# One fixed order for the whole opening, with half-height matmuls in the short convolution and the turns

## The chip, the cores and the metric

The kernel runs on one core of one Trainium2 chip. The metric is the device time of one execution in microseconds; the time of a kernel is the median over its runs. A profiled execution has its own time and a span, from its first to its last instruction.

## The reference

Two layers are applied twice to x (2048 rows, 448 columns, bf16), and then the gradients of all inputs are formed by the chain rule. Layer A turns k by a causal convolution of four taps, multiplies by v, and convolves the result with a filter as long as the sequence (by a Fourier transform of twice the length). Layer B is a feed-forward net with 1792 hidden columns.

```python
def _A_ref(q, k, v, shift_k, ssm_k, ssm_D):
    for t in range(ks):                      # ks = 4
        k_shift = k_shift + k_pad[:, t:t + S, :] * shift_k[:, ks - 1 - t][None, None, :]
    kv = k_shift * v
    ...                                      # y = irfft(rfft(kv) * rfft(ssm_k)), first S rows
    y = y + kv * ssm_D[None, None, :]
    return q * y
def _B_ref(x, w1, w2):
    return silu(x @ w1) @ w2

x = A_q
x = x + _A_ref(_layernorm(x), A_k, A_v, A_shift_k, A_ssm_k, A_ssm_D)
x = x + _B_ref(_layernorm(x), B_w1, B_w2)
x = x + _A_ref(_layernorm(x), A_k, A_v, A_shift_k, A_ssm_k, A_ssm_D)
x = x + _B_ref(_layernorm(x), B_w1, B_w2)
```

Only the factor q differs between the two uses of layer A: y is the same both times, so the kernel computes it once, ahead of everything else.

## The kernel before

Sequence rows lie as n = 16 p + j, with p the partition. `_ssm_prefix`, the opening, computes y's spectrum and its inverse; `Main` runs the layers forward and backward chunk by chunk (four chunks of 512 rows) and `_ssm_suffix` forms the gradients of k, v and the filter. The opening is the subject here. It has these steps:

- Loads, all issued by SyncE at the start: the filter (ksd, K_sb), the Fourier matrix M1sb, k (k_n), v (v_n), the first rows of x (x0c), small matrices Gsb and Gpre.
- Filter K: `k_turn` turns it with TensorE (ps_kt, copied to KAB); `k_stage1` multiplies by M1sb and copies to A1K (a half of KAB); then seven blocks (each 16 squares of 128 x 128) are turned, five by TensorE in half-height transposes (`turn`) and two by DMA transposes; `spec_k` applies the second stage (ps_s) and copies it back. Each of seven pieces of the spectrum (512 KB) is then stored (spec_K) and copied inside KAB with its halves swapped, by DMAs that GpSimd issues.
- kv: k is turned by 64 full-height transposes (ps_kT, copied to kT); `conv` forms the four-tap convolution as matmuls of kT with 112 x 112 diagonal matrices of the taps (diag, made by 16 VectorE operations from skc); ScalarE copies the result to ks, GpSimd stores it (KS_d), VectorE multiplies by v; `stage1_kv` multiplies by M1sb and copies to A1kv.
- Products: seven blocks of A1kv are turned (Z), the second stage is applied (F), VectorE multiplies with both halves of KAB (M, tile pab), TensorE goes back (V, ps_v), and the result is copied over A1kv. The spectrum of kv is stored (spec_KV), and the weights w1sb and w2sb are loaded behind it by GpSimd's queue.

Tiles of PSUM come from one ring of four (tag "A"). `k.bal` picks ScalarE or VectorE for a copy, by loads it keeps. From second-stage step 9 of K on, the order of TensorE, ScalarE, VectorE and GpSimd is written out in the string PRODUCTS: a capital is the step on TensorE (P, Z, F, V), on VectorE (M) or on GpSimd (Q), a small letter is its copy, with `a` for ScalarE and `d` for VectorE. Ahead of that the scheduler of the framework orders each engine's queue, and instructions of one engine run in that order. The transposes of w2 by DMA (w2T) stand on SyncE's queue behind K's two DMA transposes; the inverse matrix (Minvsb) and the first gradient rows (gb) stand behind them.

Behind the opening, `ys` multiplies A1kv by Minvsb (ps_y, 16 rows in 8 pairs, copied to Ysb), and the forward pass begins. In the suffix ksf reads KS_d back for the product of line 1340.

Of the kernel before, what the change touches and what calls it, by code (L numbers as in the profile page):

```python
# [17 lines left out]
P = 128  # L18
S = 2048
D = 448  # L20
# [101 lines left out]
PRODUCTS = """  # L122
P9 P10 P11 P12 p9a p10d p11a P13 p12d P8 p8a Z0 Q5 p13d Z1 z0d Z2 z1a Q6 F0 z2d F1 f0a F2 f1d F3 f2a F4 Q4 M0 F5 f3a Z4
f4a Z6 z4d f5a z6d F8 f8a F9 M1 F12 F13 f9a Z5 M2 f12a V0 z5d f13a Z3 v0a F11 z3yd z3xd F7 f11a M3 F6 f7a F10 V1 M4 f6a
V2 f10a M6 V3 v1a M5 V4 v2a M11 V5 v3a V6 M10 v4a V11 M12 v5a V10 M13 v6a V12 v11a M7 V13 v10a M8 V7 v12a M9 V8 v13a v8d
V9 v7a v9a
# [16 lines left out]
def kernel(  # L143
# [33 lines left out]
    k.KS_d = dram.tile([2, P, J, D // 2], BF16, name="KS_d")  # L177
# [87 lines left out]
def _fft_inv_stage2_half(k, pa, pb, B1, ci, psum, cnd):  # L265
    nc = k.nc
    pv = psum.tile([P, 2, 8, 64], FP32, name="ps_v", **k.pt["v"])
    for i in range(8):
        for src, g, first in ((pa, G_IAC, True), (pb, G_IBC, False)):
            for r in range(2):  # L270
                ri = slice(64 * r, 64 * r + 64)
                nc.tensor.matmul(pv[:, r ^ (ci & 1), i, :], lhsT=src[ri, i * P:(i + 1) * P], rhs=k.Gsb[ri, g, ri], start=first, stop=not first)  # L272
    out = (B1[:, :, 32 * ci:32 * ci + 32].rearrange("p q (i h s) -> p h i q s", h=2, s=2) if cnd
           else B1[:, 8 * ci:8 * ci + 8, :].rearrange("p i (q h s) -> p h i q s", h=2, s=2))
    _copy(nc, k.bal.pick(1024), out, pv[:].rearrange("p h i (q s) -> p h i q s", s=2))
# [43 lines left out]
def _ln_steps(k, pool, c, src, si, n_g):  # L319
# [4 lines left out]
    for tl in range(4):  # L324
        k.tc.keep_in_program_order(nc.vector.bn_stats(out=st[:, tl, :], in_=src(tl)))
# [5 lines left out]
        yield  # L331
    for tl in range(4):
        k.tc.keep_in_program_order(nc.vector.tensor_scalar(out=n_g[:, tl, :], in0=src(tl), scalar1=mv[:, tl, 0:1], scalar2=r[:, tl:tl + 1], op0=ALU.subtract, op1=ALU.mult))
        yield
# [6 lines left out]
def _ssm_prefix(k):  # L341
# [4 lines left out]
    with ExitStack() as es:  # L346
# [6 lines left out]
        k.M1sb = k.wk.tile([P, 16, 2, P], BF16, name="M1sb", tag="WX")  # L353
# [8 lines left out]
        kT = k.wk.tile([DC, 4, ND, 4, 129], BF16, name="kT", tag="W1")  # L362
        w2o = k.wk.tile([P, 2 * S + ND * 4 * DC], BF16, name="ksd", tag="W2")
        ksb = [w2o[:, i * S:(i + 1) * S] for i in range(2)]
        ksb += [_hd(k, [P, S], "K_sb")[:] for i in range(2)]
        diag = w2o[:DC, 2 * S:].rearrange("p (c j d) -> p c j d", c=ND, j=4)
        kn = k.wk.tile([P, J, D], BF16, name="k_n", tag="WY")
        vn = k.wk.tile([P, J, D], BF16, name="v_n", tag="WB")
        skc = spec.tile([DC, ND, 4], FP32, name="skc")
        skb = spec.tile([DC, ND, 4], BF16, name="skb")  # L370
# [3 lines left out]
        nc.scalar.dma_start(out=skb[:], in_=k.A_shift_k.rearrange("(c p) j -> p c j", p=DC))  # L374
        m1f = k.M1sb[:].rearrange("p a c k -> p (a c k)")
        for h in range(2):
            for lo, hi in KPARTS[2 * h:2 * h + 2]:
                nc.sync.dma_start(out=ksb[lo // P][:hi - lo], in_=k.A_ssm_k[lo:hi, :])
            nc.sync.dma_start(out=m1f[:, 2048 * h:2048 * h + 2048], in_=k.m1_h.ap()[:, 2048 * h:2048 * h + 2048])
# [17 lines left out]
        nc.gpsimd.tensor_copy(skc[:], skb[:])  # L397
        def k_turn(lo, hi):
            n = hi - lo
            kview = ksb[lo // P][:n].rearrange("p (n1 n2) -> p n2 n1", n2=16)  # L400
            pt = psum.tile([P, 2, 1024], BF16, name="ps_kt", **a_)
            pv = pt[:, :, 0:8 * n].rearrange("p g (i d) -> p g i d", d=n)
            for i in range(16):
                nc.tensor.transpose(pv[:, i // 8, i % 8, :], kview[:, i, :], k.ident[:n, :n])
            for g, e in enumerate((nc.vector, nc.scalar)):
                last = _copy(nc, e, Kt[:, 8 * g:8 * g + 8, lo:hi], pv[:, g])
                bal.add("act" if g else "dve", 0.9 if g else 0.69)
                if g == 0:
                    k.kt_copy = last

        def k_stage1(lo, hi, pairs):
            for n2 in pairs:
                ps = psum.tile([P, 2, 2, 256], FP32, name="ps_s1", **k.pt["s1"])
                if n2 == 0:
                    nc.vector.tensor_tensor(out=Kt[0:1, 0, lo:hi], in0=Kt[0:1, 0, lo:hi], in1=Drow[:, lo:hi], op=ALU.add)
                for w in range(2):
                    for c in range(2):
                        nc.tensor.matmul(ps[:, w, c, :hi - lo], lhsT=k.M1sb[:, n2 + w, c, :], rhs=Kt[:, n2 + w, lo:hi], start=True, stop=True)
                _copy(nc, bal.pick(4 * (hi - lo)), A1K[:, lo // 2:hi // 2, :, n2:n2 + 2, :].rearrange("p b c w s -> p w c b s"),
                      ps[:, :, :, :hi - lo].rearrange("p w c (b s) -> p w c b s", s=2))  # L420

        for lo, hi in ((0, 256), (256, D)):
            for plo, phi in KPARTS[lo // P:lo // P + 2]:
                k_turn(plo, phi)
# [1015 lines left out]
```

## Time and profile before

| what | value |
|---|---|
| time, median of 3 runs | 695.63 us (693.44 to 697.43) |
| the profiled execution | 692.97 us, span 690.9 us |
| busy share of the span | PE 97%, PEld 52%, DVE 70%, ACT 62%, POOL 15% |
| granted TensorE clock | 0.999 |
| chain that ended last, by engine | PE 64%, DVE 19%, issue 6%, ACT 5%, DMA 3%, POOL 3% |

PE is TensorE, PEld its loading of weights, DVE is VectorE, ACT is ScalarE, POOL is GpSimd, SP is SyncE (SPq: the queue of DMAs that it issues). A row of the groups gives line, engine, operation, out<-in, shape and count, then the busy time in us and the mean of one in ns, then the idle time ahead of it and what ended it. A row of the windows gives for each engine its busy time in the stretch, then the granted clock, the busy share of the DMA engines and GB/s. A row of the DMA issues gives the count, the KB of each and the median us from issue to landing. Matmuls overlap, so for them the busy time of a group divided by its count is the pace, and the mean is the time from start to end of one.

### The profile page before, as it was taken

The page shows a single profiled execution, that of the slowest core. Times are in us where ns is not written, and L with a number is a line of the kernel's source. Part 1 is how long each engine was busy: PE and PEld are TensorE (multiplying, and loading weights), DVE is VectorE, ACT ScalarE, POOL GpSimd, SP SyncE. Part 2 cuts the span into 40 slices and gives each one's busy share as a digit, 9 for nine tenths or more (in the row PEclk, how much of TensorE's full clock was granted, in tenths as well). Part 3 has the DMA queues.
Part 4 walks back from the last instruction along what each step waited for, and adds up shares of the span by engine and source line. Part 5 has one row for each costly group of instructions (what it writes and reads, how often), then busy time and mean ns, then how long its engine had stood idle before and what let it go on. Part 6 is the DMA issues. An engine that isn't in the chain of part 4 may idle for free.

```text
span 690.9 us, 14461 instructions
## 1 busy us (share of the span) xinstructions
PE 669.0 (97%) x5844; PEld 362.1 (52%) x5879; DVE 481.6 (70%) x1131; ACT 429.9 (62%) x522; POOL 104.8 (15%) x177
## 2 busy tenths in 40 slices
PE   8999999899999999999999999999999999999997
PEld 6876745454434444444444444544555555555666
DVE  5779943667889858899478874843936555538992
ACT  5988976878947868669577585223543543554431
POOL 1057310110011100111001000010111211102311
PEclk9999999999999999999999999999999999999999
DMA  8999978179698777597766789949599988957991
GB/s 320 244 316 321 337 203 220 56 191 259 167 265 233 221 182 176 137 253 219 199 157 183 211 231 354 271 142 210 191 249 342 328 285 315 341 190 223 320 310 42
DMA packets 203956, 162.60 MB, mean 235 GB/s; under 512 B 153505, under 2 KB 184244, under 8 KB 203122
## 3 DMA queue, kind: packets, MB, share of 16 engines
q1 hardware_dynamic: 190806, 113.35, 60.2%
q0 software_dynamic: 11088, 39.84, 16.7%
q10 hardware_dynamic: 1996, 8.49, 3.7%
q8 instruction: 46, 0.75, 0.5%
q14 instruction: 20, 0.16, 0.1%
HBM read 66.05 MB, written 54.60 MB: 175 GB/s over the span
## 4 chain that ended last, share of the span: by engine, by line
PE 64%; DVE 19%; issue 6%; ACT 5%; DMA 3%; POOL 3%; POOLq 0%; ACTq 0%
PE ps_d L1082 25%; PE ps_n L872 8%; PE ps_h L674 6%; PE ps_g L674 6%; PE ps_o L834 5%; DVE ln_st L308 2%; DVE lb_v L1030 2%; PE ps_v L272 2%; POOL rstd L313 2%; DMA spec_K<-KAB 1%; DVE n L316 1%; DVE lb_v L1033 1%; DVE lb_v L1034 1%; DVE X L838 1%; PE ps_h L678 1%
## 5 line engine op out<-in xcount | busy, mean ns | idle before, releaser
L1082 PEld LDWEIGHTS <-dstat 128*128 128x128 bf16 x928 | 87.1, 98 | 75.7 <-issue 4.0
L872 PE MATMUL ps_n<-w1T,ghT 128*128 128x448 bf16 x448 | 96.6, 353 | 2.0 <-DVE ghT L857 1.7
L834 PE MATMUL ps_o<-w2sb,aT 128*128 128x448 bf16 x448 | 89.2, 353 | 0.6 <-DVE X L838 0.6
L674 PE MATMUL ps_h<-nT,w1sb 128*128 128x512 bf16 (+1 forms) x410 | 83.5, 336 | 2.2 <-ACT Dall L116 1.0
L116 ACT CAST ghT<-ps_g 128x1024 bf16<-128x1024 f32 (+1 forms) x54 | 48.4, 900 | 58.3 <-PE ps_g L678 47.7
L674 PE MATMUL ps_g<-nT,w2T 128*128 128x512 bf16 x317 | 77.9, 379 | 2.2 <-DVE Dall L117 0.5
L872 PEld LDWEIGHTS <-ghT 128*128 128x128 bf16 x448 | 41.4, 98 | 50.7 <-DVE ghT L857 6.7
L834 PEld LDWEIGHTS <-aT 128*128 128x128 bf16 x448 | 43.2, 98 | 41.1 <-issue 2.7
L674 PEld LDWEIGHTS <-w1sb 128*128 128x128 bf16 x420 | 39.2, 98 | 36.7 <-issue 7.2
L817 ACT ACTIVATE aT<-ps_h 128x1024 bf16<-128x1024 f32 (+1 forms) x48 | 44.2, 921 | 19.1 <-PE ps_h L674 10.2
L1030 DVE SCALAR_TENSOR_TENSOR lb_v<-lb_u,n 128x448 bf16<-128x448 bf16 x60 | 37.2, 620 | 24.5 <-ACT lb_u L876 24.1
L116 ACT CAST Dall<-ps_h 128x1024 bf16<-128x1024 f32 (+2 forms) x60 | 54.3, 904 | 0.0
L313 POOL TENSOR_TENSOR rstd<-ln_ve,mhalf 128x2 f32<-128x2 f32 (+1 forms) x24 | 19.9, 831 | 225.7 <-DVE ln_ve L312 225.7
L674 PEld LDWEIGHTS <-w2T 128*128 128x128 bf16 x336 | 31.3, 98 | 42.1 <-issue 7.2
L827 ACT ACTIVATE Dall<-Dall 128x1024 bf16<-128x1024 bf16 (+1 forms) x48 | 53.2, 1186 | 0.1
L1082 PE MATMUL ps_d<-X,dstat 128*128 128x448 bf16 x224 | 47.6, 353 | 0.0
L1082 PE MATMUL ps_d<-go,dstat 128*128 128x448 bf16 x224 | 47.2, 353 | 0.0
L1082 PE MATMUL ps_d<-n3m,dstat 128*128 128x448 bf16 (+1 forms) x240 | 47.0, 340 | 0.0
L1082 PE MATMUL ps_d<-n1m,dstat 128*128 128x448 bf16 (+1 forms) x240 | 46.5, 340 | 0.0
L876 ACT ACTIVATE lb_u<-ps_n,rstd 128x448 bf16<-128x448 f32 x32 | 20.5, 640 | 28.9 <-PE ps_n L872 24.3
L116 ACT CAST A1g<-ps_v 128x1024 bf16<-128x1024 f32 x14 | 15.0, 1069 | 36.5 <-PE ps_v L272 36.5
L838 DVE TENSOR_TENSOR X<-X,ps_o 128x448 bf16<-128x448 bf16 x32 | 19.5, 611 | 21.3 <-PE ps_o L834 21.1
(210 smaller groups left out, 1112.4 us busy)
## 6 DMA issues: line engine op xcount, KB each, us to landing
dstat<-a_d SPq DMA_DIRECT2D x28, 512.0 KB, 5.2
dstat<-g_d SPq DMA_DIRECT2D x28, 512.0 KB, 5.8
a_d<-turned SPq DMA_DIRECT2D x16, 512.0 KB, 3.0
g_d<-turned SPq DMA_DIRECT2D x16, 512.0 KB, 3.0
a_d<-turned SPq DMA_DIRECT2D x16, 384.0 KB, 2.7
g_d<-turned SPq DMA_DIRECT2D x16, 384.0 KB, 3.0
spec_K<-KAB POOLq DMA_DIRECT2D x7, 512.0 KB, 5.7
KAB<-KAB POOLq DMA_DIRECT2D x28, 128.0 KB, 5.1
```

The lines of the kernel that those rows point to most:

```text
L116: return nc.scalar.copy(out, in_)
L272: nc.tensor.matmul(pv[:, r ^ (ci & 1), i, :], lhsT=src[ri, i * P:(i + 1) * P], rhs=k.Gsb[ri, g, ri], start=first, stop=not first)
L313: nc.gpsimd.tensor_tensor(out=r[:, lo:hi], in0=ve[:, lo:hi], in1=k.mhalf[:, lo:hi], op=ALU.pow)
L674: self.nc.tensor.matmul(ps, lhsT=w[:, b, ft * P:(ft + 1) * P], rhs=x[:, b], start=(start and b == 0), stop=(stop and b == bs[2]))
L817: self.last_silu = nc.scalar.activation(aT[hh][:, o:o + hi - lo, :], ps(lo, hi), ACT.Silu)
L827: self.nc.scalar.activation(dT[hh][:, o:o + n, :], dT[hh][:, o:o + n, :], ACT.Derivative_silu)
L834: nc.tensor.matmul(po[:, :D], lhsT=aT[ft // 7][:, ft % 7, tl * P:(tl + 1) * P], rhs=self.w2sb[:, ft, :], start=(ft == 0), stop=(ft == NF - 1))
L838: self.last_o = nc.vector.tensor_tensor(out=X[:, t, :], in0=X[:, t, :], in1=po[:, :D], op=ALU.add)
L872: nc.tensor.matmul(pn[:, :D], lhsT=gh[ft // 7][:, ft % 7, tl * P:(tl + 1) * P], rhs=self.w1T[:, ft, :], start=(ft == 0), stop=(ft == NF - 1))
L876: nc.scalar.activation(u0[:], pn[:, :D], ACT.Identity, scale=k.rstd[2 * L + 1][:, t:t + 1], accum_out=cp[:, tl, 0:1])
L1030: nc.vector.scalar_tensor_tensor(out=v[:], in0=u0, scalar=-1.0 / D, in1=n_t, op0=ALU.mult, op1=ALU.mult, accum_out=cp[:, 1:2])
L1082: self.nc.tensor.matmul(ps[:, cols], lhsT=st[:, t, :], rhs=mov[:, t, cols], start=(first and t == 0), stop=(last and t == NT - 1))
```

## The change

The whole opening, from the first turn of the filter on, is written out in one list, OPENING, that fixes the order on TensorE, ScalarE, VectorE, GpSimd and SyncE and names the copying engine; `k.bal` is not asked there any more. With it:

- k is turned in blocks of 128 columns (GBLK: 0, 128, 256 and 320 to 448) instead of 112; an `h` behind T, K, Z or V means pairs of half-height (64-row) transposes or matmuls instead of full ones. Two of four turns of k, all seven of K, six of seven of kv and three of fourteen inverse steps are half.
- The convolution uses 64 x 64 diagonals on half the rows at a time, in columns 0 to 256 and 256 to 448 (CH) instead of two halves of 224; the diagonals are made by two VectorE products (`G_`).
- All seven K blocks are turned by TensorE. KD, a DMA transpose, is defined but not in the list.
- On SyncE's queue w2T, Minvsb and gb have only the loads ahead of them.
- Copies of the first turns (a) and of k's turns (t) are whole or half as listed; stores of kv's spectrum (U) stand where the list has them.
- KS_d is stored as [P, J, D]: runs of 256 or 192 columns instead of 4 x 224; ksf is loaded and used in that form.

```diff
-PRODUCTS = """
-P9 P10 P11 P12 p9a p10d p11a P13 p12d P8 p8a Z0 Q5 p13d Z1 z0d Z2 z1a Q6 F0 z2d F1 f0a F2 f1d F3 f2a F4 Q4 M0 F5 f3a Z4
...
+OPENING = """
+A0 a0xd A1 a1xd a1ya B01 a0yd b01a G0 G1 B03 b03a A2 a2d B02 A3 D0 B06 b06d B04 b02a a3a B15 b15d B17 T1 t1d b04a T0
+t0d b17a B16 b16a B05 b05a T2h D1 t2d C01 c01a B10 b10d B11 b11a O01 C02 c02a O02 m01 T3h t3d B07 b07a B14 b14a C12
+c12a O12 B13 m02 B00 C03 b00a N0 b13d N1 B12 c03a S011 s011a S020 b12d m12 K0h k0d O03 s020a S021 K1h S120 S010 s021a
+k1d s120a s010a C13 c13a O13 S121 P2 p2a N2 N3 C10 s121d c10a K4h P3 p3a m03 S031 K3h k4d P1 m10 P0 Q1 s031a k3d N4
+p1a p0a m13 C00 c00a O00 K2h P7 K5h p7a N5 k2d S030 k5d P4 P6 s030a S101 Q0 C11 p4a m00 S001 p6d Q3 s101a c11d S100
+s100d P9 S000 s001a p9a s000d P11 p11a S131 s131a O10 O11 K6h k6d m11 S130 s130a P8 p8a Z2h z2d P12 p12a Z1h P13 p13a
+z1d S111 s111d P10 p10a N6 Q4 N7 S110 Z0h z0d Z3h s110a P5 Q6 Z6h z3xa z3yd p5a Q2 F2 f2a F7 z6d M2 F4 F6 f6d F13 f7a
+M7 f4a F12 F0 f13a U13 F1 W1 W2 W4 W0 Q5 M6 f12a f0a Z5 f1a V7 Z4h v7a z5d F3 f3a z4d U6 M13 V2 v2a F10 f10a F9 f9a F5
+M3 f5a V6 U4 v6a F8 f8a U7 M12 V13 v13a F11 f11a M1 U2 V3h U0 v3a V12 M4 V1 M9 M0 V4 V0 v12a M11 v1a v4a v0a V9h V11
+M5 v9a V5 M10 U11 V10 M8 V8h v11d v5a v8a v10d U9
 """
...
+        def G_(r):
+            n, rs = 3 + r, slice(64 * r, 64 * r + 64)
+            nc.vector.tensor_tensor(out=diag[rs, 0:n].rearrange("p c j d -> p (c j) d"),
+                                    in0=k.ident[rs, rs].rearrange("p (o d) -> p o d", o=1).broadcast_to((64, 4 * n, 64)),
+                                    in1=skb[rs, 0:n].rearrange("p c (j o) -> p (c j) o", o=1).broadcast_to((64, 4 * n, 64)), op=ALU.mult)
...
+        def C_(h, jq):
+            pc = bank(("c", h, jq), [P, 4, 4, 64], "ps_cv")
+            at = {(0, 0): 0, (0, 1): 2, (1, 0): 1, (1, 1): 3} if h == 0 else {(2, 0): 1, (2, 1): 2, (3, 1): 3}
             for u in range(4):
                 j = 4 * jq + u
...
+                for e in (2 * h, 2 * h + 1):
+                    for q in range(4):
+                        js = (j - q) % J
+                        src = kT[:, js // 4, e, js % 4, 1:129] if j >= q else kT[:, js // 4, e, js % 4, 0:128]
+                        for r in range(2):
+                            if (e, r) in at:
+                                rs = slice(64 * r, 64 * r + 64)
+                                nc.tensor.matmul(pc[:, at[e, r], u, :], lhsT=src[rs], rhs=diag[rs, e, q, :], start=(q == 0), stop=(q == 3))
...
+        def W(i):
+            if i == 0:
+                k.gb0 = _hd(k, [P, 4, D], "gb0")
+                nc.sync.dma_start(out=k.gb0[:], in_=_pm(k.grad_out[0])[:, 0:4, :])
+            elif i == 1:
+                k.w2T = k.wk.tile([P, ND, F], BF16, name="w2T", tag="WY")
+                nc.sync.dma_start_transpose(out=k.w2T[:, 0:3, :], in_=k.B_w2[:, 0:384])
+            elif i == 2:
+                nc.sync.dma_start_transpose(out=k.w2T[:, 3:4, :], in_=k.B_w2[:, 320:448])
+            else:
+                _load_minv(k, nc.sync)
...
+        with tc.manual_schedule(engines={e.engine for e in (nc.tensor, nc.scalar, nc.vector, nc.gpsimd, nc.sync)}):
+            for tok in OPENING.split():
...
-                ksf = sp.tile([P, 2, J, D // 2], BF16, name="ksf")
+                ksf = sp.tile([P, J, D], BF16, name="ksf")
```

A filter step is A (turn), B (stage 1), D (adds ssm_D), K (turn), P (stage 2), Q (store and swaps); a kv step is G (diagonals), T (turn of k), C (convolution), O (store), m (product with v), S (stage 1), Z, F, U, M, V as above; N is the first layer norm, W is on SyncE. The digits name column half, row group or block; x and y halve a copy.

More of the change, by code (lines that the diff above doesn't have):

```diff
@@ new lines, in turned @@
+        def turned(key, name, srcs, half):
+            if half:
+                pt = bank(key, [P, 2, 16, 64], name, BF16)
+                for i in range(16):
+                    _turn64(k, pt, i, srcs(i))
+                live[key] = pt[:].rearrange("p r i x -> p i r x")
+            else:
+                pt = bank(key, [P, 16, P], name, BF16)
+                for i in range(16):
+                    nc.tensor.transpose(pt[:, i, :], srcs(i), k.ident[:])
+                live[key] = pt[:].rearrange("p i (r x) -> p i r x", r=2)
@@ L537, in Q, with Z_ @@
             _swap_halves_dma(k, KAB[:, 0, :], Ka, lo, hi)
[L539 to L546 removed]
+        def Z_(g, half):
+            turned(("z", g), "ps_tr", lambda i: B1[:, 16 * g + i, :], half)
```

318 lines of the change are left out of this document (147 added, 171 removed).

## The prediction

> **What bounds the kernel now.** I read the page first, then the chain of waits, then the busy time by stretch, then the groups by form. The program computes the opening (both spectra, their product, the inverse) and then a long feed-forward part in which TensorE never stops. The diff touches the opening and two lines far behind it, so the question is when the opening ends and whether that moves the end.
>
> ```profile
> span 690.9 us, 14461 instructions
> ```
> ```profile
> 83.71 1.02 ACT A1kv L116
> 84.77 0.93 PE ps_y L599 x4
> ```
> The chain shows the handover: the last inverse copy into A1kv ends at 84.7 us and ps_y starts at once. Every product feeds every output row, so nothing of ps_y can start before it; behind it the chain runs through ps_y, ps_g, ps_h without a wait for a transfer. An earlier copy moves the end by as much.
>
> ```profile
> core 0: us, PE busy (x) PEld busy (x) DVE busy (x) ACT busy (x) POOL busy (x), PEclk, DMA share, GB/s
> 7.30:20.00 12.70, 10.81 (x124) 9.46 (x122) 11.38 (x17) 10.66 (x12) 0.00 (x0) 1.00 1.01 389
> 20.00:52.20 32.20, 29.45 (x550) 25.82 (x551) 24.69 (x50) 27.99 (x30) 11.56 (x21) 1.00 1.15 268
> 52.20:83.70 31.50, 29.52 (x381) 22.80 (x384) 30.64 (x29) 28.43 (x30) 18.58 (x35) 1.00 0.99 326
> sum 76.40, PE 69.78 PEld 58.08 DVE 66.70 ACT 67.08 POOL 30.14; mean PE 23.26 PEld 19.36 DVE 22.23 ACT 22.36 POOL 10.05
> ```
> No engine alone bounds these 76.4 us: TensorE is busy 69.8, VectorE 66.7, ScalarE 67.1. But the stretches differ. From 52.2, where the order is already written out by hand (PRODUCTS), VectorE idles 0.9 us of 31.5 (97% busy). From 20.0 to 52.2, where the scheduler orders convolution, stage 1 and turns, it idles 7.5 of 32.2 (77%), ScalarE 4.2. That idle time is the prize, with whatever work disappears.
>
> **The change part by part.** TensorE first.
>
> ```profile
> L467 PE MATMUL ps_cv<-ksd,kT 112*128 112x112 bf16 x256 | 13.9, 213 | 0.4 <-ACT KAB L116 0.3
> L272 PE MATMUL ps_v<-Gsb,pab 64*128 64x64 bf16 x896 | 15.5, 190 | 0.0
> L448 PE MATMUL ps_kT<-ident,k_n 128*112 128x128 bf16 x64 | 3.7, 219 | 0.0
> L542 PE MATMUL ps_tr<-ident,A1kv 128*128 128x128 bf16 x112 | 7.1, 219 | 0.3 <-ACT KAB L116 0.2
> L232 PE MATMUL ps_tr<-ident,KAB 64*128 64x64 bf16 x160 | 2.9, 190 | 0.0
> ```
> The convolution loses 256 full-height matmuls (13.9 us) and gains 4 x (64 + 48) = 448 of half height, the shape of L272, accumulating as those do: 15.5/896 = 0.0173 each, 7.8 us. So -6.1. k's turns go from 64 transposes (3.7) to 32 full and 64 half: 1.9 + 1.2, -0.6. K's go from 160 half ones to 7 x 32 = 224 at 0.018, +1.1. Six of seven kv turns become half: 16 at 0.063 + 192 at 0.018 = 4.5 for 7.1, -2.6. Three inverse steps of 16 full matmuls (1.0 at L542's rate) become 32 half ones (0.55), -1.3. In all -9.5, and 60.3 left of 69.8.
>
> VectorE and ScalarE share the copies out of PSUM; the new list names the engine of each, so I count its entries by the rows' means.
>
> ```profile
> L117 DVE CAST KAB<-ps_s 128x1024 bf16<-128x1024 f32 x10 | 12.0, 1221 | 1.6 <-PE ps_cv L467 1.2 <-PE ps_s L418 0.4
> L117 DVE CAST KAB<-ps_s 128x768 bf16<-128x768 f32 x4 | 3.7, 953 | 0.1
> L116 ACT CAST KAB<-ps_s 128x1024 bf16<-128x1024 f32 x12 | 12.1, 1041 | 1.2 <-PE ps_s L251 0.7 <-PE ps_s L483 0.2 <-PE ps_s L418 0.2
> L116 ACT CAST KAB<-ps_s 128x768 bf16<-128x768 f32 x4 | 3.2, 874 | 0.2 <-PE ps_s L418 0.2
> L117 DVE CAST A1kv<-ps_s 128x896 bf16<-128x896 f32 x7 | 7.5, 1083 | 0.5 <-PE ps_s L483 0.5
> L116 ACT CAST A1kv<-ps_s 128x896 bf16<-128x896 f32 x9 | 8.5, 978 | 0.0
> L117 DVE COPY KAB<-ps_tr 128x2048 bf16<-128x2048 bf16 x2 | 2.4, 1214 | 1.0 <-PE ps_tr L232 1.0
> L116 ACT COPY KAB<-ps_tr 128x2048 bf16<-128x2048 bf16 x3 | 5.5, 1887 | 0.0
> L117 DVE COPY kT<-ps_kT 112x1024 bf16<-112x1024 bf16 x4 | 2.6, 682 | 0.0
> L116 ACT COPY kT<-ps_kT 112x1024 bf16<-112x1024 bf16 x4 | 3.8, 1023 | 0.4 <-PE ps_kT L448 0.4
> L117 DVE COPY KAB<-ps_kt 128x1024 bf16<-128x1024 bf16 x3 | 2.1, 692 | 6.6 <-PE ps_kt L404 6.5
> L116 ACT COPY KAB<-ps_kt 128x1024 bf16<-128x1024 bf16 x3 | 3.0, 1012 | 6.1 <-DVE KAB L117 6.1
> L470 ACT CAST ks_kv<-ps_cv 128x896 bf16<-128x896 f32 x8 | 7.3, 914 | 3.8 <-PE ps_cv L467 3.6
> L431 DVE TENSOR_SCALAR ksd<-ident,skc 112x112 bf16<-112x112 bf16 x16 | 2.8, 242 | 0.0
> L1324 DVE TENSOR_TENSOR wx<-wx 128x896 f32<-128x896 bf16 x16 | 16.8, 1077 | 0.0
> L720 DVE TENSOR_TENSOR a_t<-n,Ysb 128x896 bf16<-128x896 bf16 x14 | 8.6, 619 | 0.1
> ```
> VectorE: K's stage-1 copies 4+4 become 1 of 1024 and 4 of 768, 3 x 1.22 fewer, -3.7; kv's 7 x 1.08 become 1 + 3, -3.5; K's stage-2 copies 6 become 1, 5 x 1.22, -6.1; K's turns 2 become 7, 5 x 1.21, +6.1; kT's four half copies become four whole ones, 4.9 - 2.6, +2.2; the first turns, whose 64-wide fourth part counts half, +0.9; one convolution copy +0.95; one inverse copy +1.2; one kv half turn becomes whole, +0.5. The 16 diagonal products (2.8) become two over 768 and 1024 elements, for which there is no like row: 1.2 at L720's rate, 2.1 at L1324's; I take 2.1, since the second operand is spread by repetition, and it costs the sum 0.9 at most. -0.7. Total about -2.1.
> The Trainium skill ("VectorE: DVE Perf Modes", What auto-detection actually checks) lets the fast mode run only where every tensor steps by one element; that operand steps by none, so by the page it is the upper value, and no run here shows it yet. By it the sum stands; by the lower one VectorE would have 0.9 less.
> ScalarE: stage 1 of K +3 x 1.04, of kv 7 x 1.04 + 5 x 0.87 for 9 x 0.98, +2.8; stage 2 of K 8 become 13, +5.2; K's turns -3 x 1.89; kT -3.8; the first turns -1.5; the convolution 4 x 1.04 + 3 x 0.87 for 7.3, -0.5; one kv turn halved -0.9; one inverse copy -1.0. Total about -2.3.
> So VectorE needs 64.6, ScalarE 64.8, TensorE 60.3 of what were 76.4 us.
>
> How densely will that run? The first 12.7 us wait for loads as now: 11.4 of VectorE's work. The products part, 30.6, keeps 31.5. The remaining 22.6 run at between 77% (29.4) and 97% (23.3); I take the middle, 87%, 26.0. Sum 70.2, against 76.4: **-6.2**. Ends: -9 and -3. The list fits such packing: its running sums for VectorE and ScalarE stay within some 3 us up to its middle, and the copy that frees a PSUM bank is always listed ahead of the matmuls four banks on.
>
> Transfers. SP loses K's two DMA transposes, and w2's, behind them, go as soon as TensorE has turned k, near 20 us instead of 27.
>
> ```profile
> 20.48 6.46 SPq L442 DMA_TRANSPOSE KAB<-KAB  x2
> 27.04 6.83 SPq L452 DMA_TRANSPOSE w2T<-in_B_w_dram  x1
> ```
> ```profile
> 42.67 0.54 POOL L492 DMA_DIRECT2D spec_K<-KAB  x1 [1.54 <-ACT ks_kv L470]
> ...
> 76.11 1.11 POOL L567 DMA_DIRECT2D w2sb<-in_B_w_dram  x1 [0.57 <-DMA spec_KV<-ZkvA]
> ```
> ```profile
> w2sb<-in_B_w_dram POOLq DMA_DIRECT2D x1, 1568.0 KB, 16.2
> ```
> ```profile
> q0 software_dynamic: 3704, 12.97, 99.2%
> ```
> The last row is the queue of GpSimd's transfers from 45 to 85 us: 99.2% of the engines. So transfers are the hidden second bound. The first of them, 42.67 now, is listed behind some 25 us of VectorE's work, near 35 us; it moves ahead with the rest, and so does the last. GpSimd keeps its order: each KS_d store, seven rounds of store and swaps, eight kv stores. A late one holds all behind it, but each product is listed 9 us of VectorE's work or more behind its swap. The later ksf load and its product change layout only: nothing counted.
>
> Sum: 692.97 (span 690.9 and 2.1 around it) - 6.2 = 686.8. That run lies 2.7 below the median 695.63; on the median's footing it is **689.4**.
>
> **The rivals.** *No denser than now* (0.15): the list meets delays its author didn't foresee, or the full queue sets the pace, and the stretch keeps its present 9.7 us of VectorE idle: 64.6 + 9.7 = 74.3, -2.1, 693.5. For it: the 99.2%. Against: PRODUCTS ran at 97% beside the same queue.
> *Given back at the handover* (0.04): the weights for ps_o come last on GpSimd's list. Now they are issued 8.6 us ahead of the copy's end and land 7.6 behind it; if the issue slips by what ps_o has in hand, ps_o starts when it does now and most is lost: 695.
> *Late loads, slower* (0.10): the early w2 transposes overtake the tail of the loads.
>
> ```profile
> x0c<-in_A_q_dram SPq DMA_DIRECT2D x1, 448.0 KB, 15.4
> 7.78 0.33 SPq L385 DMA_DIRECT2D x0c<-in_A_q_dram  x1
> GB/s 0 0 180 137 230 327 431 406 328 311 393 366 229 229 447 430 392 459 401 430 395 430 392 411 411 449 363 382 308 202 27 113 290 261 60 38 290 421 163 273
> ```
> x0c lands at 23.2; its norm is listed behind 16 us of VectorE's work, near 24. The rate row (0.75 us a slice, to 30 us) falls to 27 to 113 GB/s once transposes run. Were 0.9 MB still out, at 70 GB/s they would take 13 us; all of VectorE's list stands behind the norm: -6.2 + 12 = +6, 701.5. It decides if x0c lands after 31 us. Against: the transposes of 20.48 met the same tail and the loads, issued ahead, came through.
> *The clock* (0.03): TensorE's share falls from 91% to 86%, in short waits. If its clock fell by half for a third of the work, 60.3 would be 80; with none to all of TensorE's present 6.6 idle the end comes 4 to 10 us later than now, 703. Against: the granted clock is 1.00 in every stretch above, idle or not. The Trainium skill ("TensorE: Matmul & The Clock Gate", A second HAM failure mode: psum-queue depth-cycling) tells of such a loss between bursts into cycled PSUM banks; the trace so far doesn't show it.
>
> **How the numbers follow.** 0.5%, 3.5 us, is about what a measurement of this kernel tells from no change. The forecast has 0.68. Faster: that and a small part of the first rival, 0.70; same: the rest of it and the handover, 0.17; slower: 0.13. The range starts at -9 less the runs' own spread of some 2 (684.5) and ends past the first two rivals (697); left out are the slower cases and a little below, some 0.17.
>
> **What would show it.** Right: VectorE and ScalarE at over 90% from 20 us to the first ps_y, which starts near 78.5; the new convolution near 7.8 us of TensorE; two diagonal products near 2.1 together; w2T issued near 20; the first spec_K near 35; the stretches behind ps_y unchanged. Wrong: VectorE idle in blocks behind a load, a PSUM bank or a swap; ps_o waiting for its weights; a granted clock under 1.00.

## The result and the profile after

The changed kernel takes 698.02 us (median of 22 runs, 695.02 to 701.32) against 694.19 us for the kernel before in the same session (22 runs, 693.07 to 697.43): a ratio of 1.0047, 95% interval [1.0031, 1.0063]. The forecast was 689.4 us. The profiled execution took 699.18 us, of which 697.2 us are span, 6.3 us more than before.

Busy time by stretch of the changed kernel (from and to, length, then for each engine busy time and count, the granted clock, the busy share of the DMA engines, GB/s):
```profile
7.30:20.00 12.70, 8.92 (x116) 7.38 (x116) 9.66 (x12) 8.30 (x9) 0.00 (x0) 1.00 1.02 349
20.00:52.20 32.20, 23.76 (x735) 18.40 (x736) 20.97 (x31) 21.57 (x25) 9.78 (x14) 0.89 0.86 219
52.20:83.70 31.50, 28.48 (x556) 21.04 (x561) 30.48 (x30) 31.27 (x36) 21.34 (x41) 1.00 0.96 301
20.00:30.00 10.00, 8.67 (x337) 7.52 (x333) 7.43 (x11) 7.42 (x9) 2.33 (x3) 1.00 1.01 252
30.00:40.00 10.00, 3.97 (x74) 2.71 (x74) 2.31 (x4) 3.20 (x4) 0.75 (x1) 0.66 1.13 241
40.00:50.00 10.00, 9.02 (x309) 6.82 (x312) 9.02 (x15) 8.75 (x10) 4.99 (x7) 1.00 0.46 162
70.00:80.00 10.00, 8.65 (x158) 6.88 (x157) 9.85 (x10) 10.00 (x13) 6.74 (x13) 1.00 0.94 288
```
The first three rows answer to those of before. The middle stretch, where the gain was to be, fell from 77% to 65% of VectorE's time; the last one kept 97%. The first one lost too: 9.7 us of VectorE's work by 20 us instead of 11.4. The largest loss sits in one place: from 30 to 40 us VectorE works 2.3 us of 10, TensorE 4.0, and the granted clock, 1.00 in all three stretches of before, is 0.66.

The timeline of TensorE (start, busy time of the group, line and operation, count, idle time ahead and its releaser; "issue": nothing that the profile shows) has two long standstills there:
```profile
26.07 1.11 PE L506 MATMUL ps_cv<-M1sb,kT 64*128 64x64 bf16 x47 [1.33 <-issue]
36.10 0.82 PE L531 MATMUL ps_s<-ks_kv,M1sb 128*128 128x256 bf16 x3 [6.03 <-issue]
```
Each lies in the middle of a step, with operands and bank at hand. The three matmuls behind the second take 0.82 us. How many TensorE instructions went ahead of each standstill (the same kind of row, from the start):
```profile
0.00:24.73 24.73, 19.77 (x351) 14.93 (x351) 14.17 (x17) 13.17 (x15) 2.65 (x11) 1.00 0.90 302
0.00:30.07 30.07, 23.77 (x479) 18.28 (x479) 17.93 (x24) 17.28 (x20) 4.06 (x12) 1.00 0.95 284
```
351 and 479: 128 matmuls and 128 weight loads apart, 256 instructions. The page's list of DMA queues has a queue of instructions (packets, MB, share of the engines); below are that row and TensorE's of after, then both of before:
```profile
PE 663.7 (95%) x6274; PEld 353.6 (51%) x6311; DVE 480.5 (69%) x1113; ACT 426.7 (61%) x522; POOL 106.5 (15%) x176
...
q8 instruction: 49, 0.80, 0.5%
```
```profile
PE 669.0 (97%) x5844; PEld 362.1 (52%) x5879; DVE 481.6 (70%) x1131; ACT 429.9 (62%) x522; POOL 104.8 (15%) x177
...
q8 instruction: 46, 0.75, 0.5%
```
(6274 + 6311)/49 = 257 and (5844 + 5879)/46 = 255: each packet, 0.80 MB/49 = 16 KB, brings about 256 of TensorE's instructions. Of the DMA queues by stretch in the changed kernel, 26.5 to 30 and 30 to 33 us have no packet of this queue; 33 to 36.2 us has one:
```profile
q8 instruction: 1, 0.02, 3.0%
```
3.0% of 16 engines over 3.2 us are 1.5 us for one packet: in the trace it starts at 33.15 us and has landed at 34.70, and TensorE goes on at 36.10, 1.4 us later. Behind the first standstill it is the same: a packet from 23.63 to 24.74, TensorE at 26.07. So the program of TensorE is itself a transfer, and here it came late. The clock fell while TensorE stood (the last number but two is the granted clock):
```profile
30.00:33.00 3.00, 0.07 (x1) 0.00 (x0) 0.98 (x2) 1.12 (x2) 0.75 (x1) 1.00 1.21 196
33.00:36.20 3.20, 0.10 (x1) 0.10 (x2) 0.00 (x0) 0.00 (x0) 0.00 (x0) 0.52 1.09 160
```

The second loss is at the handover, again from the timeline:
```profile
87.78 1.68 PE L642 MATMUL ps_y<-A1kv,Minvsb 128*128 128x448 bf16 x8 [0.38 <-ACT A1kv L116]
91.81 1.71 ACT L643 CAST Ysb<-ps_y 128x896 bf16<-128x896 f32 x2 [4.08 <-DMA spec_KV<-ZkvB]
92.77 1.73 PE L642 MATMUL ps_y<-A1kv,Minvsb 128*128 128x448 bf16 x8 [3.30 <-ACT Ysb L643]
```
ps_y starts 3.0 us later than before (84.77), and its copies then wait until the last stores of KV's spectrum have left the memory that Ysb takes over: 3.3 us more. (That memory is ZkvA's, though the row names ZkvB: in the trace its last store landed at 91.64 us, before at 80.26.) 3.0 + 3.3 is the whole difference of the spans.

GpSimd's timeline tells why they are late, first after, then before:
```profile
73.73 0.78 POOL L567 DMA_DIRECT2D w1sb<-in_B_w_dram  x1
...
76.92 0.54 POOL L562 DMA_DIRECT2D spec_KV<-ZkvA  x1 [1.85 <-ACT ZkvA L116]
...
80.59 1.06 POOL L562 DMA_DIRECT2D spec_KV<-ZkvB  x2 [0.25 <-ACT ZkvB L116]
```
```profile
73.56 0.78 POOL L561 DMA_DIRECT2D w1sb<-in_B_w_dram  x1
...
75.00 0.54 POOL L556 DMA_DIRECT2D spec_KV<-ZkvB  x1
```
The new list puts w1's load behind the second store (U6): six stores follow it, the last issued at some 81 us. Before, one store followed, at 75.00.

### The profile page after: what moved, and what is told of

Same layout as the page of the kernel before. It is cut to its first block, busy times and chain, and to the rows that moved or that the text cites. A ratio compares the mean times of both kernels' runs of the same rounds, so it can differ in the third digit from the quotient of the medians.

```text
span 697.2 us, 15286 instructions
## 1 busy us (share of the span) xinstructions
PE 663.7 (95%) x6274; PEld 353.6 (51%) x6311; DVE 480.5 (69%) x1113; ACT 426.7 (61%) x522; POOL 106.5 (15%) x176
## 4 chain that ended last, share of the span: by engine, by line
PE 63%; DVE 17%; issue 7%; ACT 6%; DMA 5%; POOL 2%; SPq 0%; ACTq 0%; DVEq 0%; POOLq 0%
PE ps_d L1125 25%; PE ps_n L915 8%; PE ps_h L717 6%; PE ps_o L877 5%; PE ps_g L717 5%; DVE ln_st L319 3%; DVE lb_v L1073 2%; DMA k_n<-in_A_k_dram 2%; PE ps_v L278 2%; DMA spec_KV<-ZkvB 2%; POOL rstd L324 2%; DVE n L327 1%; DVE lb_v L1076 1%; DVE lb_v L1077 1%; DVE X L881 1%
```

## The experiments

The theories named in the expectations: F, TensorE's instruction fetch, itself a transfer, comes late beside w2's DMA transposes and the loads; T, any transfer of that size does it; D, the order waits by itself; I, the number of TensorE instructions; W, w2's early transposes alone; H, the handover. The ratios are to the kernel before on the same chip; "stands" are idle times of TensorE put down to issue, of over 0.5 us, from 20 to 50 us (1.33, 6.03 and 0.56 in the change); a few came later and are told below.

| run | edit to the changed kernel | us | ratio [95%] | stands, us |
|---|---|---|---|---|
| e1_w2_late | w2's transposes held back | 729.37 | 1.0442 [1.0398, 1.0486] | 2.79 |
| e2_w2_plain | w2T by plain loads | 693.85 | 0.9965 [0.9943, 0.9987] | 3.02 |
| e3_full | no half-height turns or inverse steps | 694.06 | 0.9977 [0.9952, 1.0001] | 1.75, 2.02 |
| e4_before_kturn | kernel *before*, K blocks by TensorE | 694.68 | 0.9972 [0.9954, 0.9991] | none |
| g1_tk_full | only the turns of k and K full | 695.13 | 0.9989 [0.9963, 1.0016] | 0.92, 3.66 |
| g2_conv_full | convolution in full rows | 695.09 | 0.9982 [0.9959, 1.0005] | none |
| g5_w1_last | w1's load behind the stores | 694.61 | 0.9982 [0.9955, 1.0009] | 1.39, 4.94 |
| g8_three | g1, g5 and skb's second load on GpSimd | 693.33 | 0.9959 [0.9935, 0.9984] | 0.92, 3.94 |
| h1_extra192 | g2 and 192 one-column matmuls | 706.26 | 1.0151 [1.0117, 1.0185] | none |
| h2_conv_three | g2, g5 and skb's second load on GpSimd | 691.88 | 0.9939 [0.9919, 0.9958] | none |
| h3_few | h2 and the turns of k and K full | 693.51 | 0.9977 [0.9956, 0.9998] | none |
| h4_e3_three | e3, g5 and skb's second load on GpSimd | 694.43 | 0.9977 [0.9952, 1.0002] | 1.24, 2.84 |
| i1_slow_pace | half matmuls row group by row group | 697.61 | 1.0026 [1.0003, 1.0049] | 0.83, 4.13, 0.96 |
| i3_late_half | h2, last four convolution blocks in halves | 692.48 | 0.9954 [0.9933, 0.9974] | 2.21, 1.00 |
| i5_skb | skb's second load on GpSimd alone | 696.49 | 1.0008 [0.9983, 1.0034] | 1.57, 4.94 |
| j1_e_outer | h2, loops of a convolution step exchanged | 690.82 | **0.9925 [0.9902, 0.9947]** | none |
| j2_w2_mid | g5, skb's second load, w2's transposes behind `k1d` | 699.03 | 1.0040 [1.0020, 1.0060] | 2.52, 1.90 |

**e1_w2_late.** A copy of four elements of k_n, from which w2T takes its memory over, is listed behind `z3yd`; w2's transposes have to wait for it. Minvsb and gb go ahead.
```diff
-... W1 W2 W4 W0 Q5 ...        -... Z6h z3xa z3yd p5a ...
+... W1 W2 Q5 ...              +... Z6h z3xa z3yd X0 p5a ...
```


> The changed kernel with w2's two DMA transposes held back until the last kv turn but two (a copy of four elements of k keeps k's buffer taken until then); Minvsb and gb go ahead of them. Theory F (TensorE's instruction fetch, itself a transfer, stands behind the DMA transposes): the standstill of 6.0 us at 30 us and the half clock after it are gone, no TensorE gap marked issue is over 1.5 us before 55 us, ps_y starts at 78 to 82 instead of 87.8; the transposes now share the full queue of spectra, so some of it is lost at the handover: 687 to 693 us. Theory D (the new order itself waits there, whatever w2 does): standstill stays, 697 to 700 us.

The stand after matmul 479 was gone; one of 2.79 us appeared after matmul 351, at 23.6 us, in the tail of the loads. What was lost instead came from the transposes, now beside GpSimd's full queue (SyncE's timeline of e1, then of after):
```profile
57.83 25.02 SPq L610 DMA_TRANSPOSE w2T<-in_B_w_dram  x1
82.91 8.77 SPq L612 DMA_TRANSPOSE w2T<-in_B_w_dram  x1
```
```profile
23.77 7.65 SPq L610 DMA_TRANSPOSE w2T<-in_B_w_dram  x1
31.46 3.81 SPq L612 DMA_TRANSPOSE w2T<-in_B_w_dram  x1
```
They held SyncE for 33.8 us instead of 11.5, and the swaps and stores beside them slowed down until TensorE had waited 33.6 us for pab, in four waits, before ps_y. Late is far worse than early, and the expected 687 to 693 us was missed.

**e2_w2_plain.** The same bytes by plain loads; w2's turn is left out.
```diff
-nc.sync.dma_start_transpose(out=k.w2T[:, 0:3, :], in_=k.B_w2[:, 0:384])
+nc.sync.dma_start(out=k.w2T[:, 0:3, :]..., in_=k.B_w2...[:, 0:3 * F])
```


> The changed kernel with w2's two DMA transposes replaced, at the same place on SyncE's queue, by two plain loads of the same 1.6 MB (the turn of w2 is left out, w2T holds unturned rows). Theory F with the transposes as the cause: standstill and half clock gone, ps_y near 79 to 81, 686 to 691 us. Theory T (any transfer of that size at that time holds up the fetch): a standstill of 3 to 6 us stays, 693 to 698. Theory D: no change, 697 to 700.

The stand after matmul 479 stayed, at half its length:
```profile
32.37 0.82 PE L531 MATMUL ps_s<-ks_kv,M1sb 128*128 128x256 bf16 x3 [3.02 <-issue]
```
So transfers as such can do it (T); beside the transposes it was twice as long.

**e3_full** takes the `h` off every T, K, Z and V. **e4_before_kturn** gives the kernel before the K turns of the change, with w2's transposes right behind k's turn.
```diff
-... B05 b05a T2h D1 ...        -            if g < 5:
+... B05 b05a T2 D1 ...         +            if g < 7:
```

> The changed kernel with every turn and inverse step full height (no h in the list): half as many instructions in 18 steps, more time in each; convolution and w2's transposes stay. Theory F: the convolution alone still runs through 256 instructions in some 2 us while the transposes run, so a standstill of 4 to 7 us stays, TensorE has 4 us more work: 697 to 702 us. Theory I (the sheer number of TensorE instructions, not the transposes): standstill under 3 us, 691 to 695.

> The kernel before with one part of the change alone: all seven K blocks turned by TensorE, so that w2's transposes follow k's turn at once. Theory F: w2's transposes at 23 us meet the old convolution (64 instructions in 1.75 us, half the rate); gaps marked issue of 2 to 4 us as before, the two blocks add 3 us of copies partly in idle time: 693 to 697 us. Theory W (w2's early transposes alone cost the 6 us, whatever TensorE's list): a gap of 5 us or more, 698 to 701.

e3 has the list, the order and w2's transposes of the change, and is not slower than before: D falls. Its stands come after weight loads 479 and 607. F had expected 697 to 702 us and missed; the time and the length of each stand came as theory I had them, so I stayed open until h1. e4 issues w2's transposes at 22.70 us and shows no stand: that part of the change cost no time by itself, and W falls.

**g1_tk_full, g2_conv_full.** Two ways to fewer TensorE instructions. In g2 the diagonals are made at full height, and a step is one matmul of 128 rows instead of two of 64:
```diff
-for r in range(2):
-    if (e, r) in at:
-        nc.tensor.matmul(pc[:, at[e, r], u, :], lhsT=src[rs], rhs=diag[rs, e, q, :], ...)
+nc.tensor.matmul(pc[:, u, o:o + w], lhsT=src[rs], rhs=diag[rs, e, q, rs], ...)
```


> The changed kernel with its early turns (k and the K blocks) at full height, 16 TensorE instructions for a block instead of 32; the turns of Z and V late in the opening stay in halves. Theory F (TensorE runs out of instructions when many small ones meet full DMA engines): 144 instructions fewer around 10 to 60 us, so the standstill of 6.0 us shrinks to 3 us or less, the clock granted in 30-40 us is over 0.9, and the time is 693 to 695 us, as with every turn at full height (694.1). Theory L (the late half turns are what cost, by their own number): 697 to 698 us, the early gap gone or not. Theory D (the order waits by itself): 698 us with the gap in place.

> The changed kernel with the convolution in full rows (256 matmuls of 128 rows instead of 448 of 64) and the diagonals in full rows; the turns stay in halves. Theory F: the 448 half matmuls are the largest group of small instructions ahead of the standstill, so with 192 fewer the standstill shrinks to under 3 us and the time is 693 to 697 us, though TensorE has some 5 us more of work by rows. Rival (only the half turns outrun the fetch, the convolution does not): the standstill stays at about 6 us and the time is 698 to 703 us.

g1 only moved the stand: 0.92 us after matmul 479, 3.66 us one block later. g2 took it away (the rows of g2 by stretch):
```profile
20.00:30.00 10.00, 10.00 (x175) 9.11 (x173) 6.13 (x11) 6.92 (x8) 2.33 (x3) 1.00 0.83 219
30.00:40.00 10.00, 9.77 (x191) 7.17 (x190) 7.62 (x12) 7.94 (x10) 2.55 (x3) 1.00 1.19 192
```
There TensorE works without a break, and the clock stays at 1.00. But one stand came far behind, among the products, where no transpose runs and GpSimd's transfers fill the DMA engines; it stands after weight load 1247 (351 + 7 x 128):
```profile
81.20 0.23 PE L267 MATMUL ps_v<-Gpre,pab 128*128 128x128 bf16 x1 [1.49 <-issue]
```

**g5_w1_last, g8_three.** w1's load moves from U6 to U9, behind the last store, ahead of w2sb's:
```diff
-            if lo == 6:
+            if lo == 9:
```


> The changed kernel with w1's load moved behind all stores of KV's spectra on GpSimd's queue; nothing else. Theory H (the handover pays 3.3 us because the last spectra stores queue behind w1's 0.4 MB while the first stage after the opening waits for them): the waits on spec_KV before Ysb and X shrink from 4.1 and 1.0 us to 1 us or less, and the time is 694 to 696 us with the early standstill unchanged at about 6 us. Rival (the stores are late by their own issue time, or the software queue's total sets it): the waits stay and the time is 697 to 699 us.

> Three edits to the changed kernel together: the turns of k and the K blocks at full height, the second of the diagonals' two loads on GpSimd's queue (so that k's and v's loads are issued at the times they had before), and w1's load behind the stores of KV's spectra. If the three losses named by theories F (standstill), H (handover) and the late loads are separate, they add up: standstill under 2 us, loads of k landed by 17 us, the wait at Ysb under 1.5 us, 688 to 692 us. If what is won early is given back at the handover, 693 to 696 us.

g5: the first copy to Ysb runs at 87.6 us, 1.0 us behind ps_y, and the wait for spec_KV is gone from both places, with the stand still at 4.94 us. The handover is shown to be w1's place. g8 missed: its stands hold 4.86 us, its clock fell as well, and the three gains did not add up.

**h1_extra192.** Ahead of each sum's first matmul stand three of one column and 64 rows, overwritten at once.
```diff
+for x in range(3):
+    nc.tensor.matmul(pc[:, u, o:o + 1], lhsT=src[rx], rhs=diag[rx, e, 0, rx.start:rx.start + 1], start=True, stop=True)
```

> The kernel with the convolution in full rows (which had no standstill) plus 192 one-column matmuls before the real ones, so that the opening again issues as many TensorE instructions as the changed kernel; the columns are overwritten, nothing else differs. At the 17 ns of a half matmul the 192 are 3.3 us of TensorE work. Theory F (instructions are fetched in blocks of 256, and blocks used up faster than they arrive beside full DMA engines leave TensorE standing): TensorE stands still again for 1.5 us or more, and exactly after its 351st or 479th matmul, and the time is 695 to 699 us. Rival R (it was the half rows themselves, their row groups or their diagonals): no standstill above 0.8 us, and 693 to 697 us from the added work alone.

Both expectations failed: no stand, and 706 us. An extra matmul cost 48 ns (ps_y 9.2 us later for 192), so the pace did not rise: matmuls 352 to 479 took 8 us. It still tells one thing: with as many convolution matmuls as the change (448) TensorE did not stand. The number as such (I), which e3 had left open, is not it.

**h2_conv_three, h3_few, h4_e3_three.** All three have g5's edit and this one:
```diff
-nc.scalar.dma_start(out=skb[64:128, 3, :], in_=k.A_shift_k[384:448, :])
+nc.gpsimd.dma_start(out=skb[64:128, 3, :], in_=k.A_shift_k[384:448, :])
```

> Convolution in full rows, turns in halves, the second load of the diagonals on GpSimd's queue and w1's load behind the stores of KV's spectra. If the handover (2.3 and 1.1 us at Ysb in the kernel with the convolution alone) is again a matter of w1's place, ps_y starts at about 85.5 us without a wait behind it: 690 to 692 us. If the two gains cover the same time, 692.5 to 694 us.

> The same with the early turns (k and the K blocks) at full height as well: 144 TensorE instructions fewer. Theory F has nothing more to gain from it, since no standstill is left: the full turns add some 0.4 us of TensorE work each, up to 5 us in a stretch where TensorE is busy 9.8 of 10 us: 691 to 695 us, not faster than with half turns. Rival (the half turns still cost by their number): 688 to 691 us.

> Convolution in halves, every turn at full height (694.1 us, standstills of 1.75 and 2.02 us, no drop of the clock), the second load of the diagonals on GpSimd's queue and w1's load behind the stores of KV's spectra. If handover and late loads are separate losses: the standstills stay at 1.5 to 4 us, the wait at Ysb goes, 690.5 to 692.5 us. If the time is set before the handover: 693 to 695 us.

h2 beats both kernels. Its copies to Ysb follow ps_y (83.8 us) without a wait for a store. h3 gains nothing over it, as F says when no stand is left; TensorE is busy 10.0 of 10 us there. h4's profiled run has the shortest span of all (689.2 us), but that run is the fastest of twelve, which spread from 691.57 to 697.85. The median, 694.43, lies in the range for a time that is set before the handover; why they spread is open.

**i1_slow_pace, i3_late_half, i5_skb.** i1 makes `for r in range(2)` the outer loop of a step. i3 has the changed kernel's halves again in four blocks of h2. i5 is the edit just shown, alone.
```diff
-for e in (2 * h, 2 * h + 1):             +HALF = {(1, 3), (1, 0), (0, 0), (1, 1)}
-    for q in range(4):                   +half = (h, jq) in HALF
-        for r in range(2):
+for r in range(2):
+    for e in (2 * h, 2 * h + 1):
+        for q in range(4):
```

> The changed kernel with the same 448 half matmuls of the convolution, issued row group by row group (all of rows 0 to 63 of a step, then all of rows 64 to 127) instead of turn about; same instructions, same number, same work. In the kernel with 192 extra one-column matmuls, which lie in one row group, an extra one cost 48 ns (9.2 us later at ps_y for 192), against 17 ns of a half matmul turn about. If that is the price of not alternating, the convolution takes 10 us or more longer and a block of 256 instructions lasts 6 us or more instead of 3.5 to 4. Theory F (pace against the arrival of instruction blocks): the standstills after matmuls 351 and 479 are gone (under 0.8 us each) although nothing was taken out, granted clock 1.00, time 700 to 710 us by the slower matmuls. Rival R (the number of instructions or the half rows as such): TensorE stands 3 to 6 us after matmul 479 all the same, and the time is above 708 us.

> The fastest version so far (convolution in full rows, diagonals' second load on GpSimd's queue, w1's load last; 691.9 us) with the last four of the eight convolution blocks in halves again. They come when the loads and w2's transposes are through. By F the pace there does no harm, and TensorE, which is busy 9.9 of 10 us from 20 to 50 us, saves 0.5 to 0.65 us in each: 689.5 to 691.5 us, no standstill over 0.8 us. Rival (the fetch is outrun beside the stores too): a standstill of 1.5 us or more after 35 us, 692 to 695 us.

> The changed kernel with only the second of the diagonals' two loads moved from ScalarE's queue to GpSimd's. If the late loads (k landed at 19.8 us, x0c at 25.2) cost time by themselves: k lands 1 us earlier or more, ps_y 1 us or more earlier, 695 to 697 us. If the standstill after matmul 479 takes it up: 697 to 699 us with the gap as long or longer.

i1 did not slow the pace (matmuls 352 to 479 in 4.3 us), so it tells nothing apart. i3 does. Of h2 it changes only what comes after 33 us, and there the stands came back, again at block ends (607 and 735), as its rival had it. SyncE had issued w2's transposes by 34.4 us and the second landed at 39.9, so the first stand begins in their tail and the second comes behind them; the time, 692.48 us, can't be told from h2's:
```profile
0.00:37.98 37.98, 34.20 (x607) 27.64 (x607) 25.95 (x37) 25.19 (x28) 7.20 (x16) 1.00 1.01 271
0.00:45.38 45.38, 39.40 (x735) 31.18 (x735) 29.75 (x42) 29.54 (x33) 10.43 (x22) 0.96 0.98 279
```
i5 landed k 2 us sooner and lies between the change and the kernel before; its interval just touches the change's, so that the later loads cost something is likely and not settled.

**j1_e_outer, j2_w2_mid.** j1 exchanges two loops; j2 has the `X0` of e1 earlier.
```diff
-for u in range(4):                       -k1d s120a ...
-    for e in (2 * h, 2 * h + 1):         +k1d X0 s120a ...
+for e in (2 * h, 2 * h + 1):
+    for u in range(4):
```


> The version with the convolution in full rows, the diagonals' second load on GpSimd's queue and w1's load last (691.9 us), with the loops of a convolution step exchanged: all matmuls of 128 rows first, then all of 64 rows, instead of four and four. There 64 matmuls of 64 rows took 4.6 us, 72 ns each, and an extra one-column matmul of 64 rows among full ones 48 ns, against 17 ns for those among their like. If it is the change between the two heights that costs, TensorE saves 2 to 3 us between 30 and 50 us, where it is the bound: 689.5 to 691 us, no stand over 0.8 us although a block of 128 matmuls then lasts 6.2 us instead of 6.8. If the price lies elsewhere: 691.5 to 692.5 us as before.

> The changed kernel, all halves kept, with w1's load last and the diagonals' second load on GpSimd's queue, and w2's transposes held until K's second block is copied, at 32 to 36 us, behind the place of the stand and ahead of most of GpSimd's stores and swaps. Theory F: without them the packet for matmul 480 comes in time, the stand of 6 us there is under 1 us (the one after 351, in the tail of the loads, may stay at 1 to 3 us), the transposes take 11 to 20 us, and the time is 688.5 to 692.5 us. Rival (fetch is outrun beside whatever fills the engines, stores and swaps too): a stand of 2 us or more comes after 607 or later instead, 693 to 697 us.

j1 has the lowest time; its interval overlaps h2's, so that it is faster than h2 is not shown by the time. It is by TensorE's busy time. The groups of the convolution, of h2 and then of j1 (line, operation, shape, count, busy time, mean ns):
```profile
L506 PE MATMUL ps_cv<-M1sb,kT 128*128 128x128 bf16 x192 | 14.1, 220 | 0.1
L506 PE MATMUL ps_cv<-M1sb,kT 64*128 64x64 bf16 x64 | 4.6, 192 | 0.0
```
```profile
L506 PE MATMUL ps_cv<-M1sb,kT 128*128 128x128 bf16 x192 | 12.2, 219 | 0.2
L506 PE MATMUL ps_cv<-M1sb,kT 64*128 64x64 bf16 x64 | 2.6, 191 | 0.0
```
18.7 against 14.8 us: it is the change between full and half height that costs. j2 gives the sharpest answer on the stands, and the worst time but two. With w2's transposes at 33.81 us TensorE crossed 479 and 607 without a stand although it used its blocks up in 3.8 and 4.3 us, and the list ran as it was meant to:
```profile
30.00:40.00 10.00, 9.68 (x295) 7.42 (x296) 9.84 (x17) 9.87 (x12) 3.79 (x6) 1.00 0.71 141
```
The next stand, 1.90 us, came while they ran, after weight load 863. The stand after 351, where no transpose of w2 runs yet, stayed at 2.52 us. The expected 688.5 to 692.5 us was missed. The time was lost again by the transposes' being late: SyncE had issued them by 51 us and the second landed at 64.9, the chain of waits has 16.3 us for one swap inside KAB beside them, and one more stand came after weight load 1119:
```profile
58.62 0.26 PE L238 MATMUL ps_tr<-ident,A1kv 64*128 64x64 bf16 x5 [2.58 <-issue]
```

Put together: the time that TensorE took for one block of 128 matmuls, when the one packet of the instruction queue that comes in that block starts (counted from the block's first instruction), and how long TensorE stood behind the block.

| kernel, matmuls | block, us | packet starts at, us | stand, us |
|---|---|---|---|
| after, g5, i5: 352 to 479 | 4.0 | 7.1, 6.5, 6.6 | 6.03, 4.94, 4.94 |
| e2 (plain loads): 352 to 479 | 4.0 | 4.5 | 3.02 |
| j2 (no transposes yet): 352 to 479, 480 to 607 | 3.8, 4.3 | 1.0, 1.1 | 0 |
| j2 (transposes): 608 to 735, 736 to 863 | 5.0, 2.7 | 1.1, 1.6 | 0, 1.90 |
| j2 (transposes): 992 to 1119 | 4.6 | 4.6 | 2.58 |
| i3: 480 to 607, 608 to 735 | 4.3, 5.2 | 3.9, 3.8 | 2.21, 1.00 |
| g1, e3: 480 to 607 | 5.0 | 6.0, 4.5 | 3.66, 2.02 |
| e4: 352 to 479 | 5.1 | 2.6 | 0 |
| before: 352 to 479 | 6.1 | 2.1 | 0 |
| h2: 352 to 479, 480 to 607 | 6.8, 6.9 | 3.1, 3.0 | 0 |
| g2, h2: 1120 to 1247 | 6.2, 6.0 | 4.7, 2.1 | 1.49, 0 |

Shown: every stand lies at the end of such a block, the late ones too (weight load 1119 in j2, 1247 in g2, 1375 in g8, 1503 in e2 and i1), and in each TensorE goes on 1.2 to 2.1 us after the packet of that block has landed. So the stand is the wait for the packet: it comes where a block is used up before its packet has been there that long. A quick block makes that likely, a late packet does it even behind a block of 6.2 us (g2). Late packets came beside full DMA engines: up to the packet their busy share is 1.22 in the change (352 to 479) and 1.01 in g2 (1120 to 1247), but 0.67 in h2 in the same block of 1120 to 1247, and 0.10 in j2 from 608 on (a share can exceed 1). Not shown: when a packet is asked for, and why in e4 and h2, beside engines as full (1.27 and 1.28 from 352 on), it started after 2.6 and 3.1 us and not after 7; that it waits in line behind the others' packets is argued.

## Why the prediction was wrong

**The step that failed** is "The remaining 22.6 run at between 77% ... and 97%". Its low end was taken from the present order, as if a new list could only be as loose as the old one. TensorE entered the sum as busy time alone: halves made the convolution, K's and kv's turns cheaper by rows, and by the same stroke doubled their instructions per us. Nothing in the sum priced the supply of instructions. From 20 to 52.2 us VectorE reached 65%, which is 3.7 us below even the low end (24.7 to 21.0), and in it lie 7.9 us of standstill and 6.8 us at half clock, 2.9 of them inside the standstill. A smaller step failed ahead of it: "The first 12.7 us wait for loads as now: 11.4 of VectorE's work" held 9.7, with k landed at 19.8 us (17.8 in i5); what that cost is not settled.

**The terms.** Some held. A first-half step of the convolution takes 1.10 us for 64 matmuls, 0.0172 each (forecast 0.0173), and the two diagonal products 2.19 us against 2.1 (timeline of after):
```profile
9.00 2.19 DVE L463 TENSOR_TENSOR M1sb<-ident,skb 64x768 bf16<-64x768 bf16 x2
...
20.36 1.10 PE L506 MATMUL ps_cv<-M1sb,kT 64*128 64x64 bf16 x64
```
The latter was the higher of two prices; the Trainium skill ("VectorE: DVE Perf Modes", What auto-detection actually checks), by which an operand that doesn't step keeps the fast mode away, agrees with it. VectorE's and ScalarE's busy time over the whole span fell by 1.1 and 3.2 us (forecast 2.1 and 2.3). The products part kept its 97%. TensorE's term did not hold: its busy time fell by 5.3 us (669.0 to 663.7), not 9.5. A second-half step of the convolution takes 1.11 us for its 48 matmuls, as long as one of 64, so the convolution took 9.1 us and not 7.8; K's turns took 5.4 and not 4.0, two of the seven at half clock.

**First spec_K** was to be issued near 35 us and went at 46.81 (42.67 before); so all of GpSimd's queue came later, and the handover found its stores unfinished. w2's transposes, put near 20 us, went at 23.8.

**The rivals.** *No denser than now* was too kind. *Given back at the handover* happened, at another place: not the weights for ps_o, but w1's load ahead of six stores of the spectrum; g5 gave it back. *Late loads* did not decide: x0c landed at 25.2 us, not after 31. *The clock* came true in small, with another trigger: not short waits between bursts, but one long stand. h2 goes through the same PSUM banks in the same order at 1.00; so the rule of the Trainium skill that the prediction weighed ("TensorE: Matmul & The Clock Gate", A second HAM failure mode: psum-queue depth-cycling) is not what happened here.

**How much of the gain was there.** j1, without stand and handover, is 0.75% faster than before: 5.2 of the forecast's 6.2 us (3.7 to 6.8 by its interval). It has the list, K's turns and the halves of the turns from the change; the convolution's halves, which were to save the most on TensorE, are not in it. The busy row of j2 from 30 to 40 us tells that the list can run densely with them; what that would be worth without late transposes stays open. ps_y at 78.5 us was reached by none (83.0 in h4, 83.3 in j1).

## What to carry to other kernels

Cutting a matmul in two halves saves rows and doubles instructions: price the pace too, as us per 128 matmuls. Beside transfers that fill the DMA engines a packet started up to 7.1 us into its block here and was of use only 1.2 to 2.1 us after landing, so where 128 matmuls take some 6 us or less, expect that TensorE may stand behind them; idle time put down to "issue" in the middle of a step is recognised by counting TensorE's instructions ahead of it. A transfer that does harm where it stands may do more where it is moved to, so price both places. Stores that free memory for the next stage go ahead of loads that nobody waits for yet.

## What the runs showed of the hardware

- TensorE's instructions come in packets of 16 KB for about 256 instructions, over the same DMA engines as the data, one in each block of 128 matmuls; behind a stand TensorE goes on 1.2 to 2.1 us after the packet has landed. The Trainium skill ("Runtime: NRT & Kernel Launch", Instruction fetch mechanics) has the 256 and calls the cost of crossing a block mostly hidden; the first agrees with the counts 351, 479 and 607, the second does not hold here, where one crossing took 6.03 us.
- With the 6.03 us the clock went to half for 6.8 us (0.66 over 10 us: 0.34 x 10 x 2), from 33.15 us on, while TensorE still stood; with e2's 3.02 us likewise, and with e1's 2.79 and i3's 2.21 us for 3.4 us (i3: 0.83 over 10 us), in i3 from 1.2 us behind the stand on. e3's 1.75 and 2.02 us cost no clock, nor did h4's 2.84 or j2's 2.52. The Trainium skill ("TensorE: Matmul & The Clock Gate", The HAM clock gate) has a window of 3.4 us, and the two lengths agree with it; but a stand well under 3.4 us can be enough.
- The same DMA transposes held SyncE for 11.5 us when issued at 24 us, 17.2 at 34 us (j2) and 33.8 at 58 us (e1), beside GpSimd's queue; the second landed 7.3, 24.8 and 29.1 us after its issue.
- 64-row matmuls cost 72 ns each in h2, where four of them and four full ones take turns, 41 ns in j1, 16 in a row, 20 to 25 ns in i1 (1.27 to 1.63 us for 64) and 17 ns in the change's first-half steps, where the two row groups take turns (23 in its second-half steps, 48 in 1.11 us).
